# Strassen's scheme for four more token tiles, earlier weight sums, and a last product that ends in parts

## The chip, the cores and the metric

The kernel runs on one core of one Trainium2 chip. A core has five engines that work side by side, each through its own instruction queue: TensorE (PE, matmuls into PSUM banks), VectorE (DVE), ScalarE (ACT), GpSimd (POOL) and SyncE (SP, which here issues nearly all transfers). The metric is the device time of one execution in microseconds; of several runs the median is taken.

## What is computed

Four batches, eight heads, 768 tokens, head size 64. First comes clustered attention: each query and each key is given to the nearest of 16 centroids of its head, and a query sees the keys of its own cluster only. Then a gated feed-forward layer works on all 3072 tokens.

```python
q_assign = np.argmax(np.einsum('bhsd,hcd->bhsc', q_n, c_n), axis=-1)
k_assign = np.argmax(np.einsum('bhsd,hcd->bhsc', k_n, c_n), axis=-1)
mask = q_assign[:, :, :, None] == k_assign[:, :, None, :]
scores = np.where(mask, scale * np.matmul(q, k.transpose(0, 1, 3, 2)), -1e9)
attn_out = softmax(scores) @ v                     # (B, H, S, D)
x = attn_out.transpose(0, 2, 1, 3).reshape(B * S, H * D)
gate = 1.0 / (1.0 + np.exp(-(x @ w_gate)))         # 512 -> 1536
return gate * (x @ w_val) @ w_out                  # 1536 -> 512
```

## The kernel before

**Attention in steps.** The batches b0 to b3 follow each other. The work of attention is cut into 384 steps (96 for each batch): one score matmul of 128 keys by 384 queries (line 788), one exponential on ACT (line 793), three small matmuls into the `av` bank (line 811). Between them stand, at planned steps, what prepares the coming heads: casts and splits of q and k (lines 1353 and 1354), transposes by DMA, cluster logits (`lg`, lines 421 and 434), which DVE reduces to `lgs` (line 449) and to one-hot rows (lines 460 to 469), the sums of v (lines 330 to 346).

**The feed-forward layer as filler.** When a half batch (three token tiles of 128, a block) is through attention, its atoms go into a queue (`ffn_block`): per chunk fc of 12, a gate atom (four matmuls into a bank `g`, line 529, tanh on ACT, line 535) and a value atom (four matmuls into a bank `v`, line 545; DVE then makes the hidden tile `hT`, line 550), and after them the atoms of the output product. At each step `ffn_run(ns)` adds `ns` to a credit and takes atoms from the front of the queue while the credit is positive. The table `SCHED` gives ns for every 24 steps of a batch (`ns10` is the first quarter of batch 1); so it sets how many matmuls of the layer stand beside each step. What is left at the end runs after the last step. The banks `sc`, `g`, `v` and `lg` share a ring of four PSUM banks; two more banks (`op`) hold outputs or transposes (`turns`), two more `av`.

**The output product, plain.** For b0 (`b < PB`, PB = 1) each of the six tiles has twelve matmuls of 512 columns into one bank (line 583), a copy to SBUF on ACT (line 593, tiles 0 and 2 of a block) or DVE (line 591, tile 1) and a store of 256 KB (line 502).

**The output product by Strassen's scheme (Winograd's form).** For b1 to b3 two token tiles and the two halves of the hidden axis make a 2 x 2 block matrix, as do the halves of `w_out` on both axes. Seven products (`steps` in `product_out`) of six matmuls with 256 columns (line 716) stand for eight. It needs four sums of token blocks (class `Sums`, lines 626 to 632, on DVE, made at the chunks that `SUMS_AT` names), four sums of weights (`mix_wo`, line 276, eight instructions on DVE, which go into the held tiles of k, q, v that batch 0 no longer needs, and, last, over the upper right quarter of `w_out`), and sums of products (line 658, DVE; the first one is a copy on ACT, line 662). Two banks, x and y, take the products in turn; a product that starts afresh in a bank waits until the sum of the one before has read it. Tiles (0, 1) of a batch are one product of a single pair, made beside the second block's gates (`aside`); tiles (3, 2) and (4, 5) are one product of two pairs at the batch's end: 84 matmuls, each sum 128 x 512. The last product of the kernel (`final`) stores its parts as they come: the lower tiles, the right half, and, after the seventh product (B21, `end2`), the left half with 128 x 2 x 256.

**Order.** Each engine runs its instructions in the order in which this program issues them. The weights' sums were planned at steps 150 to 170 and 200 to 204; no Strassen product may start before them, and the last of them may not come before the plain products, which read the quarter that it overwrites.

Of the kernel before, what the change touches and what calls it, by code (L numbers as in the profile page):

```python
# [98 lines left out]
def kernel(  # L99
# [163 lines left out]
    HF, HD = NFC // 2, DM // 2  # L263
# [236 lines left out]
    def store(src, b, c0, n, m=slice(0, DM)):  # L500
        def f():
            SP.dma_start(
                out=out[b * S : (b + 1) * S].rearrange("(p c) m -> p c m", c=NCH)[
                    :, c0 : c0 + n, m
                ],
                in_=src,
            )

        d_ = SCHED.get("sd", 0)
        if d_ > 0 and b < B - 2:  # L510
            at(step_no[0] + d_, f)
        else:
            f()

    def ffn_atoms(xT, t0, n, b, final=False):
        blk = t0 // 384
        gv = []
        cost = NDC * max(n, 80) / 2.4 + 3
        pairs = [] if b < PB else [(0, 1)] if blk == 0 else [(3, 2), (4, 5)]
        sm = {x: Sums(b, *x) for x in pairs}  # L520

        def gate(fc, st):
            def f():
                need(("w", fc // WQ, 0), *(("x", b, p, t0 // 128 + c) for p in range(NP) for c in range(n // 128)))
                if fc == 0:
                    HB[b, blk] = htp.tile([128, NFC, 384], HP, name="hT")
                g = bank(512, name="g")
                for dc in range(NDC):
                    PE.matmul(  # L529
                        out=g[:, 0:n], lhsT=wg[fc // WQ][:, dc, fc % WQ, :],  # L530
                        rhs=xT[:, dc, t0 : t0 + n],
                        start=(dc == 0), stop=(dc == NDC - 1),
                    )
                th = thp.tile([128, 384], FP, name="th")
                ACT.activation(th[:, 0:n], g[:, 0:n], AF.Tanh)  # L535
                st.append(th)

            return f

        def val(fc, st):  # L540
            def f():
                need(("w", fc // WQ, 1))
                w = bank(512, name="v")
                for dc in range(NDC):
                    PE.matmul(  # L545
                        out=w[:, 0:n], lhsT=wv[fc // WQ][:, dc, fc % WQ, :],
                        rhs=xT[:, dc, t0 : t0 + n],
                        start=(dc == 0), stop=(dc == NDC - 1),
                    )
                DVE.scalar_tensor_tensor(  # L550
                    HB[b, blk][:, fc, 0:n], st[0][:, 0:n], 1.0, w[:, 0:n], ALU.add, ALU.mult
                )
                for k, x in SUMS_AT[b >= PB, blk].get(fc, []):
                    sm[x].make(k)
                if fc == NFC - 1 and pairs and blk == 0:
                    aside.extend(product_out(b, [sm[(0, 1)]], False))

            return f

        for fc in range(NFC):  # L560
            st = []
            gv.append((cost, gate(fc, st)))
            gv.append((cost, val(fc, st)))
        outs = []
        if b < PB:
            for t in range(n // 128):
                outs += plain_out(b, blk, t)
        elif blk == 1:
            outs = product_out(b, [sm[x] for x in pairs], final)
        return gv + outs  # L570

    def plain_out(b, blk, t):
# [3 lines left out]
        def outp(part):  # L576
# [22 lines left out]

    PB = 1  # L600
    SUMS_AT = {
        (False, 0): {}, (False, 1): {},
        (True, 0): {5: [(3, (0, 1))], 11: [(1, (0, 1)), (2, (0, 1))]},
        (True, 1): {
            1: [(1, (3, 2))], 5: [(2, (3, 2)), (3, (3, 2))], 6: [(3, (4, 5))],
            11: [(1, (4, 5)), (2, (4, 5))],
        },
# [26 lines left out]
    def product_out(b, sums, final):  # L634


        P_ = len(sums)
        st = {}

        def begin():  # L640
            need(*(("wo", i) for i in range(WOP)), *(("wt", i, c) for i in range(4) for c in range(2)))
            slot = taken["op"] % 2
            u = [out_bank() for _ in range(2)]
            x = 0 if slot != taken["last"] else 1
            taken["last"] = (slot + x) % 2
            taken["pair"] = True
            for z, t in (("x", u[x]), ("y", u[1 - x])):
                st[z] = t[:, 0 : P_ * HD].rearrange("p (e m) -> p e m", m=HD)
            if P_ == 1:
                ob = osp.tile([128, 2, DM], FP, name="ob")  # L650
                st["o1"], st["o2"] = ob[:, 0:1], ob[:, 1:2]
            else:
                st["o1"] = osp.tile([128, 2, DM], FP, name="ob")
                st["o2"] = osp.tile([128, 2, DM], FP, name="ob")
            for o in ("o1", "o2"):
                st[o, 0], st[o, 1] = st[o][:, :, 0:HD], st[o][:, :, HD:DM]

        plus = lambda dst, a, z: DVE.tensor_tensor(dst, a, z, ALU.add)  # L658
        C11, C12, C21, C22 = ("o1", 0), ("o1", 1), ("o2", 0), ("o2", 1)

        def end1():
            ACT.activation(st[C11], st["x"], AF.Copy)

        def end4():
            plus(st[C21], st["y"], st[C11])

        def end6():
            plus(st[C12], st["x"], st[C11])

        def end5():  # L670
            plus(st[C22], st["y"], st[C11])
            for m in sums:
                m.make(4)

        def end7():
            plus(st[C21], st["x"], st[C21])
            plus(st[C22], st["x"], st[C22])
            for i, m in enumerate(sums):
                store(st["o2"][:, i], b, m.t2, 1)

        def end3():
            plus(st[C12], st["y"], st[C12])
            if final:
                store(st[C12], b, sums[0].t1, P_, slice(HD, DM))

        def end2():
            plus(st[C11], st["x"], st[C11])
            taken["pair"] = False
            if final:
                store(st[C11], b, sums[0].t1, P_, slice(0, HD))  # L690
            else:
                store(st["o1"], b, sums[0].t1, P_)

        steps = [
            ("x", lambda m: tok(b, m.t1, 0), B11, True, end1),
            ("y", lambda m: tok(b, m.t2, 1), T4, True, end4),
            ("x", lambda m: m.of[2], T2, True, end6),
            ("y", lambda m: m.of[1], T1, True, end5),
            ("x", lambda m: m.of[3], T3, False, end7),
            ("y", lambda m: m.of[4], B22, False, end3),  # L700
            ("x", lambda m: tok(b, m.t1, 1), B21, True, end2),
        ]
        atoms = []
        G = SCHED.get("og", 3)

        def atom(k, e, g):
            z, lhs, rhs, start, end = steps[k]

            def f():
                if k + e + g == 0:  # L710
                    while aside and P_ > 1:
                        aside.pop(0)[1]()
                    begin()
                a = lhs(sums[e])
                for c in range(g, g + G):
                    PE.matmul(  # L716
                        out=st[z][:, e], lhsT=a[:, c, :], rhs=rhs[:, c, :],
                        start=start and c + e == 0, stop=c == HF - 1, skip_group_check=True,
                    )
                if g + G == HF and e == P_ - 1:  # L720
                    end()

            return f

        for k in range(7):
            for e in range(P_):
                for g in range(0, HF, G):
                    atoms.append((G * (HD / 2.4 + 2.5), atom(k, e, g)))
        return atoms

    queue = []
# [609 lines left out]
        plan(f"wo{i}", 44 + 6 * i, lambda i=i: load_wo(i))  # L1341
    for i in range(4):
        for c in range(2):
            plan(f"wt{i}{c}", (150 + 8 * i if i < 3 else 200) + 4 * c, lambda i=i, c=c: mix_wo(i, c))

    def pair_prep(b, p, use):
        st = {}
# [138 lines left out]
```

## Time and profile before

| what | value |
|---|---|
| median of 3 runs (lowest to highest) | 324.65 us (324.54 to 325.34) |
| the profiled execution's own time | 324.9 us |
| its span, first to last instruction | 323.1 us |
| busy in the span | PE 314.7, ACT 231.1, DVE 226.7, POOL 108.6 us |
| granted TensorE clock | 1.0 throughout |
| moved over DMA | 45.15 MB |

PE is the matmul side of TensorE, PEld its weight loads, which run beside the matmuls. A row of a group gives line, engine, operation, result and sources, shape and count; after the bar stand the busy time and the mean of one in ns; after the second bar the engine's idle time just before these instructions and what ended most of it. A matmul's mean holds its whole passage, so that following matmuls overlap; how far apart they start is read from the timeline. In a row of the windows each engine has its busy time in that stretch and, in brackets, its number of instructions. "SPq" are the instructions by which SP issues transfers.

### The profile page before, as it was taken

To read this page: it belongs to the slowest core of one execution; us is meant where nothing else is said; L and a number is where in the kernel's file an instruction comes from. 1 tells how busy PE (TensorE), PEld (TensorE's weight loads), DVE (VectorE), ACT (ScalarE), POOL (GpSimd) and SP (SyncE) were. 2 spreads that over 40 slices of the span, in tenths; PEclk is the share of its full clock that TensorE was granted. 3 is DMA by queue.
4 is the path that set the end of the run, shared out by engine and by line. 5 is a ranking of instruction groups with operands and counts; after the bars stand their busy time and mean duration, and the time that the engine had idled before them with its cause. 6 is when DMAs were issued, how large, how long until landed. Compare 5 with 4: busy or idle time off the path is not lost.

```text
span 323.1 us, 9150 instructions
## 1 busy us (share of the span) xinstructions
PE 314.7 (97%) x3504; PEld 222.1 (69%) x3504; DVE 226.7 (70%) x586; ACT 231.1 (72%) x520; POOL 108.6 (34%) x145
## 2 busy tenths in 40 slices
PE   7999999999999999999999999999999999999994
PEld 5888666766766656666777687666777688667683
DVE  6899656777667997576879688576867356555654
ACT  6688988787899978877867866788777876332310
POOL 5887464154335265433132352423111111000000
PEclk9999999999999999999999999999999999999999
DMA  6999995837987996974784741952503012200103
GB/s 203 384 255 189 244 164 114 200 93 222 251 122 185 159 215 155 248 197 90 107 217 115 233 101 42 311 99 52 111 2 95 34 26 79 77 2 1 67 0 130
DMA packets 77675, 45.15 MB, mean 140 GB/s; under 512 B 56832, under 2 KB 75072, under 8 KB 77632
## 3 DMA queue, kind: packets, MB, share of 16 engines
q1 hardware_dynamic: 73664, 39.73, 49.1%
q0 software_dynamic: 3680, 4.72, 8.9%
q8 instruction: 27, 0.44, 0.6%
q10 hardware_dynamic: 288, 0.13, 0.2%
q14 instruction: 16, 0.13, 0.1%
HBM read 28.34 MB, written 6.29 MB: 107 GB/s over the span
## 4 chain that ended last, share of the span: by engine, by line
PE 87%; DVE 5%; issue 3%; DMA 2%; POOL 1%; SPq 0%; ACT 0%; POOLq 0%; DVEq 0%
PE g L529 19%; PE v L545 19%; PE sc L788 17%; PE av L811 10%; PE o L716 10%; PE o L583 4%; PE lg L434 2%; PE oh_ps L1097 1%; PE lg L421 1%; PE t_ps L1037 1%; DMA xTb<-xp 1%; DMA qraw<-in_q_dram 1%; PE wm L879 1%; DVE ob L658 1%; POOL xp L375 1%
## 5 line engine op out<-in xcount | busy, mean ns | idle before, releaser
L793 ACT ACTIVATE es<-sc 128x384 f16<-128x384 f32 x384 | 174.5, 492 | 40.3 <-PE sc L788 30.9
L788 PE MATMUL sc<-T 128*128 128x384 f16 x384 | 117.8, 326 | 1.0 <-DVE lgs L449 0.6
L811 PEld LDWEIGHTS <-es 128*128 128x128 f16 x1152 | 81.3, 98 | 35.8 <-issue 0.7
L811 PE MATMUL av<-va,es 128*128 128x65 f16 x1152 | 97.5, 194 | 0.0
L550 DVE SCALAR_TENSOR_TENSOR hT<-th,v 128x384 f16<-128x384 f32 x96 | 53.1, 553 | 56.2 <-PE av L811 36.8
L529 PE MATMUL g<-xTb,wg 128*128 128x384 f16 x384 | 78.2, 326 | 0.6 <-DMA xTb<-xp 0.5
L545 PE MATMUL v<-xTb,wv 128*128 128x384 f16 x384 | 78.1, 326 | 0.0
L535 ACT ACTIVATE th<-g 128x384 f32<-128x384 f32 x96 | 47.2, 492 | 33.3 <-PE g L529 14.0
L375 POOL TENSOR_TENSOR xp<-t,rec 128x384 f16<-128x384 f32 (+1 forms) x30 | 21.8, 728 | 100.5 <-DVE rec L372 50.0
L529 PEld LDWEIGHTS <-wg 128*128 128x128 f16 x384 | 37.2, 97 | 19.7 <-issue 0.4
L545 PEld LDWEIGHTS <-wv 128*128 128x128 f16 x384 | 37.4, 98 | 19.0
L788 PEld LDWEIGHTS <-T 128*128 128x128 f16 x384 | 37.1, 97 | 0.6 <-DVE T L1118 0.5
L1354 POOL TENSOR_TENSOR hl<-kraw,hl 128x384 f16<-128x384 f32 x22 | 20.2, 920 | 42.2 <-DVE hl L1353 19.6
L658 DVE TENSOR_TENSOR ob<-o,ob 128x256 f32<-128x256 f32 (+1 forms) x42 | 22.6, 551 | 9.7 <-PE o L716 8.9
L716 PEld LDWEIGHTS <-sum 128*128 128x128 f16 x216 | 20.9, 98 | 5.6 <-DVE sum L632 0.7
L716 PE MATMUL o<-wo,hT 128*128 128x256 f16 x162 | 24.0, 272 | 0.2 <-DVE ob L658 0.2
L1354 POOL TENSOR_TENSOR hl<-qraw,hl 128x384 f16<-128x384 f32 x22 | 20.7, 940 | 10.0 <-DVE hl L1353 9.7
L370 DVE TENSOR_TENSOR t<-av,sv 128x390 f32<-128x390 f32 (+1 forms) x30 | 14.4, 479 | 8.0 <-PE av L811 7.8
L583 PE MATMUL o<-wo,hT 128*128 128x512 f16 x72 | 19.9, 379 | 0.0
L716 PEld LDWEIGHTS <-hT 128*128 128x128 f16 x162 | 15.7, 97 | 4.2 <-issue 0.4
L449 DVE TENSOR_REDUCE lgs<-lg 128x192 f32<-128x384 f32 x23 | 12.7, 551 | 2.7 <-PE lg L434 2.6
L322 POOL CAST va<-vraw 128x768 f16<-128x768 f32 x15 | 12.9, 860 | 2.5 <-DMA vraw<-in_v_dram 2.5
(140 smaller groups left out, 321.9 us busy)
## 6 DMA issues: line engine op xcount, KB each, us to landing
vraw<-in_v_dram SPq DMA_DIRECT2D x15, 384.0 KB, 5.2
kraw<-in_k_dram SPq DMA_DIRECT2D x14, 384.0 KB, 4.1
out_dram<-ob SPq DMA_DIRECT2D x20, 256.0 KB, 2.4
qraw<-in_q_dram SPq DMA_DIRECT2D x12, 384.0 KB, 4.4
wg<-in_moe_w_gate_dram POOLq DMA_DIRECT2D x2, 768.0 KB, 9.1
wv<-in_moe_w_val_dram POOLq DMA_DIRECT2D x2, 768.0 KB, 9.9
wo<-in_moe_w_out_dram POOLq DMA_DIRECT2D x2, 768.0 KB, 8.8
T<-ohT SPq DMA_DIRECT2D x44, 24.0 KB, 1.9
```

Source lines behind the costliest of these rows:

```text
L375: (eng or POOL).tensor_tensor(x, t[:, 0:nq, 0:64], bcast(rec[:, 0:nq], 64), ALU.mult)
L529: PE.matmul(out=g[:, 0:n], lhsT=wg[fc // WQ][:, dc, fc % WQ, :], rhs=xT[:, dc, t0 : t0 + n], start=(dc == 0), stop=(dc == NDC - 1),)
L535: ACT.activation(th[:, 0:n], g[:, 0:n], AF.Tanh)
L545: PE.matmul(out=w[:, 0:n], lhsT=wv[fc // WQ][:, dc, fc % WQ, :], rhs=xT[:, dc, t0 : t0 + n], start=(dc == 0), stop=(dc == NDC - 1),)
L550: DVE.scalar_tensor_tensor(HB[b, blk][:, fc, 0:n], st[0][:, 0:n], 1.0, w[:, 0:n], ALU.add, ALU.mult)
L583: PE.matmul(out=o, lhsT=HB[b, blk][:, fc, bass.ts(t, 128)], rhs=wo[fc // WON][:, fc % WON, :], start=(fc == 0), stop=(fc == NFC - 1),)
L658: plus = lambda dst, a, z: DVE.tensor_tensor(dst, a, z, ALU.add)
L716: PE.matmul(out=st[z][:, e], lhsT=a[:, c, :], rhs=rhs[:, c, :], start=start and c + e == 0, stop=c == HF - 1, skip_group_check=True,)
L788: PE.matmul(out=sc.rearrange("p (c t) -> p c t", t=128), lhsT=s["k"], rhs=s["q"], start=True, stop=True,)
L793: ACT.activation(es, sc, AF.Exp, scale=SCALE)
L811: PE.matmul(out=av[:, a0 + s["c0"] + i, :], lhsT=s["es"][:, bass.ts(i, 128)], rhs=VA[b, p][:, e, s["j"], :], start=(first and i == 0 and a ...
L1354: POOL.tensor_tensor(hl[:, :, 64:128], r, hl[:, :, 0:64], ALU.subtract)
```

## The change

Three things. First, b0 leaves the plain way after its tiles 0 and 1: tiles (3, 2) and (4, 5) go through the product of two pairs as in the other batches, and their token sums are made at the same chunks. Second, the eight weight sums are planned at steps 108, 114, ... 150, and the credits of the quarters change: 490 to 440 ns in the second half of b0, 12 ns more in all of b1, 7 to 8 less in b2. Third, in the last product of the kernel the seventh product no longer accumulates in bank x: three atoms (`closing`) take a ring bank each, for tile 3 with 256 columns and for tile 4 with two parts of 128, add them to the left half and store each part by itself.

```diff
-    300, "ns11": 280, "ns12": 290, "ns13": 265, "ns2": 600, "ns3": 350, "dm0": 7, "dm1": 2,
+    312, "ns11": 292, "ns12": 302, "ns13": 277, "ns2": 600, "ns3": 350, "dm0": 7, "dm1": 2,
...
-    -1, "b1lv1": 0.5, "b1lv2": 0.5, "b1lv3": 1.5, "ns02": 490, "ns03": 490, "ns20": 500,
-    "ns21": 491, "ns22": 481, "ns23": 491, "ns30": 443, "ns31": 443, "ns32": 443, "ns33": 423,
+    -1, "b1lv1": 0.5, "b1lv2": 0.5, "b1lv3": 1.5, "ns02": 440, "ns03": 440, "ns20": 492,
+    "ns21": 484, "ns22": 474, "ns23": 484, "ns30": 443, "ns31": 443, "ns32": 443, "ns33": 423,
...
-        pairs = [] if b < PB else [(0, 1)] if blk == 0 else [(3, 2), (4, 5)]
+        pairs = [(3, 2), (4, 5)] if blk else [] if b < PB else [(0, 1)]
...
-                for k, x in SUMS_AT[b >= PB, blk].get(fc, []):
+                for k, x in SUMS_AT[blk].get(fc, []) if pairs else []:
...
-        if b < PB:
-            for t in range(n // 128):
+        if blk == 1:
+            outs = product_out(b, [sm[x] for x in pairs], final)
+        elif b < PB:
+            for t in range(2):
                 outs += plain_out(b, blk, t)
-        elif blk == 1:
-            outs = product_out(b, [sm[x] for x in pairs], final)
...
         def end2():
             plus(st[C11], st["x"], st[C11])
             taken["pair"] = False
-            if final:
-                store(st[C11], b, sums[0].t1, P_, slice(0, HD))
-            else:
-                store(st["o1"], b, sums[0].t1, P_)
+            store(st["o1"], b, sums[0].t1, P_)
...
+        def closing(e, a, z):
+            def f():
+                o = bank(z - a, name="o_end")
+                lhs = tok(b, sums[e].t1, 1)
+                for c in range(HF):
+                    PE.matmul(
+                        out=o, lhsT=lhs[:, c, :], rhs=B21[:, c, a:z],
+                        start=c == 0, stop=c == HF - 1,
+                    )
+                m = st["o1"][:, e, a:z]
+                plus(m, o, m)
+                store(m.unsqueeze(1), b, sums[e].t1, 1, slice(a, z))
+
+            return f
+
-        for k in range(7):
+        for k in range(6 if final else 7):
             for e in range(P_):
                 for g in range(0, HF, G):
                     atoms.append((G * (HD / 2.4 + 2.5), atom(k, e, g)))
+        if final:
+            for e, a, z in ((0, 0, HD), (1, 0, HD // 2), (1, HD // 2, HD)):
+                atoms.append((900, closing(e, a, z)))
...
-            plan(f"wt{i}{c}", (150 + 8 * i if i < 3 else 200) + 4 * c, lambda i=i, c=c: mix_wo(i, c))
+            plan(f"wt{i}{c}", 108 + 12 * i + 6 * c, lambda i=i, c=c: mix_wo(i, c))
```

More of the change, by code (lines that the diff above doesn't have):

```diff
@@ L601 @@
     SUMS_AT = {
-        (False, 0): {}, (False, 1): {},
-        (True, 0): {5: [(3, (0, 1))], 11: [(1, (0, 1)), (2, (0, 1))]},
-        (True, 1): {
+        0: {5: [(3, (0, 1))], 11: [(1, (0, 1)), (2, (0, 1))]},
+        1: {
             1: [(1, (3, 2))], 5: [(2, (3, 2)), (3, (3, 2))], 6: [(3, (4, 5))],
```

## The prediction

> **What bounds the kernel now.** I read the page first, then the groups by shape, the chain of waits, the windows by stage and the timeline of the end. The page and its chain name the matrix engine:
>
> ```profile
> span 323.1 us, 9150 instructions
> PE 314.7 (97%) x3504; PEld 222.1 (69%) x3504; DVE 226.7 (70%) x586; ACT 231.1 (72%) x520; POOL 108.6 (34%) x145
> PE 87%; DVE 5%; issue 3%; DMA 2%; POOL 1%; SPq 0%; ACT 0%; POOLq 0%; DVEq 0%
> PE g L529 19%; PE v L545 19%; PE sc L788 17%; PE av L811 10%; PE o L716 10%; PE o L583 4%; PE lg L434 2%; PE oh_ps L1097 1%; PE lg L421 1%; PE t_ps L1037 1%; DMA xTb<-xp 1%; DMA qraw<-in_q_dram 1%; PE wm L879 1%; DVE ob L658 1%; POOL xp L375 1%
> ```
>
> PE is busy 97% of the span and is 87% of the chain that ended last; no other engine passes 72%. A microsecond of PE work taken out anywhere between the lead-in and the end should therefore come off the time, unless an engine that is full for a while makes PE wait. Where that can be is read from the windows; I cut them at attention steps 48, 96, 108, 132, 150, 168 and 192 (a step is one score matmul of line 788):
>
> ```profile
> core 0: us, PE busy (x) PEld busy (x) DVE busy (x) ACT busy (x) POOL busy (x), PEclk, DMA share, GB/s
> 35.80:73.30 37.50, 37.39 (x434) 25.12 (x433) 25.61 (x68) 32.44 (x75) 16.63 (x20) 1.00 0.74 160
> 73.30:80.50 7.20, 7.20 (x81) 4.46 (x80) 5.30 (x13) 5.60 (x13) 3.03 (x4) 1.00 0.79 228
> 80.50:95.20 14.70, 14.70 (x193) 10.13 (x192) 8.40 (x24) 13.13 (x31) 5.66 (x7) 1.00 0.84 184
> 95.20:104.90 9.70, 9.70 (x118) 6.59 (x117) 7.65 (x24) 8.85 (x21) 4.53 (x5) 1.00 0.96 186
> 104.90:116.30 11.40, 10.83 (x129) 7.11 (x128) 11.08 (x25) 9.40 (x23) 5.09 (x6) 1.00 0.83 176
> 116.30:129.10 12.80, 12.80 (x154) 7.98 (x152) 10.86 (x31) 10.75 (x26) 7.16 (x9) 1.00 0.80 172
> ...
> 104.90:116.30 11.40, 3.42 (x4) 1.00 0.83 176
> 116.30:129.10 12.80, 1.17 (x2) 1.00 0.80 172
> ```
>
> (The last two rows are line 276 alone, the weights' sums.) PE is full in every stretch but one. In 104.9 to 116.3 us DVE is busy 11.08 of 11.40 us, four weights' sums with 3.42 us among them, and there PE idles 0.57 us. That is the price this trace shows for a full DVE, and the waits name it:
>
> ```profile
> PE sc L788 <- DVE lgs L449: 0.6, 1, 0.6
> PE g L529 <- DMA xTb<-xp: 0.5, 1, 0.5
> PE o L716 <- DVE ob L658: 0.2, 1, 0.2
> ```
>
> **Part 1: the product of the first batch.** By the instruction order of both programs, 48 matmuls of 512 columns (line 583, four tiles of twelve) leave and 84 of 256 columns come (seven products, two tiles, six chunks). What each costs is read from spacing, since the mean of a matmul holds its whole passage through the array:
>
> ```profile
> 68.38 0.86 PE o L583 x4
> 69.75 0.86 PE o L583 x4
> ...
> 311.96 1.47 PE L716 MATMUL o<-qheld,sum 128*128 128x256 f16 x12
> 313.27 1.47 PE L716 MATMUL o<-kheld,sum 128*128 128x256 f16 x12
> ```
>
> Four wide ones take 0.86 us, 0.215 each. Twelve narrow ones start 1.31 us before the next twelve, 0.109 each. So 48 x 0.215 = 10.3 us go and 84 x 0.109 = 9.2 us come: **-1.17 us** of PE work. The 36 further weight loads lie beside the matmuls: a load takes 97 to 98 ns (groups below), less than the 109 ns of a narrow matmul. Exposed, they would cost 36 x 0.098 = 3.5 us; that is a rival.
>
> The Trainium skill, "TensorE: Matmul & The Clock Gate", section "Back-to-back issue gap", speaks against this part: it gives a sustained 131 ns for 512 columns and 81 ns for 128, by which 48 wide ones cost 6.3 us and 84 short ones at least 6.8, so the product would lose 0.5 us or more instead of gaining. The rows here do not bear it out (0.215 us for a wide one in the interleaved stretch).
>
> The other engines' share, by groups:
>
> ```profile
> L658 DVE TENSOR_TENSOR ob<-o,ob 128x512 f32<-128x512 f32 x21 | 14.1, 688 | 9.6 <-PE o L716 8.9 <-ACT es L793 0.7
> L550 DVE SCALAR_TENSOR_TENSOR hT<-th,v 128x384 f16<-128x384 f32 x96 | 53.1, 553 | 56.2 <-PE av L811 36.8 <-PE v L545 18.8
> L716 PEld LDWEIGHTS <-sum 128*128 128x128 f16 x216 | 20.9, 98 | 5.6 <-DVE sum L632 0.7
> L626 DVE TENSOR_TENSOR sum<-hT 128x768 f16<-128x768 f16 x9 | 5.9, 650 | 0.2
> L628 DVE TENSOR_TENSOR sum<-sum,hT 128x768 f16<-128x768 f16 x9 | 5.5, 606 | 0.3
> L630 DVE TENSOR_TENSOR sum<-hT 128x768 f16<-128x768 f16 x9 | 5.2, 576 | 0.1
> L632 DVE TENSOR_TENSOR sum<-hT,sum 128x768 f16<-128x768 f16 x9 | 4.7, 550 | 0.0
> L593 ACT ACTIVATE ob<-o 128x512 f32<-128x512 f32 x4 | 2.4, 600 | 0.2
> L591 DVE COPY ob<-o 128x512 f32<-128x512 f32 x2 | 1.4, 688 | 0.0
> L276 DVE TENSOR_TENSOR qheld<-wo,kheld 128x768 f16<-128x768 f16 x2 | 1.2, 584 | 0.0
> L276 DVE TENSOR_TENSOR wo<-wo,qheld 128x768 f16<-128x768 f16 x2 | 1.1, 552 | 0.0
> ```
>
> ACT loses three copies and gains one (-1.2 us). DVE gains seven sums of outputs and eight of tokens and loses one copy: 6 x 0.688 + 2 x (0.650 + 0.606 + 0.576 + 0.550) = +8.9 us, in steps 107 to 191. On SP four stores of 256 KB become two of 256 and one of 512 KB; behind the last stand transposes and loads for the next batch, issued tens of steps ahead, so a late store costs nothing there.
>
> **Part 2: the weights' sums earlier, the pace.** Eight sums move from steps 150 to 204 to steps 108 to 150. They must come before the new product starts at step 158; their inputs are ready (the second half of the weights long loaded, the held tiles free after the first quarter, the last plain output at step 107). The changed pace moves 6,144 columns of gate and value work out of steps 48 to 96, into steps 96 to 192: PE work that changes place. It costs something only where another engine then ends last. In 35.8 to 73.3 us PE's 37.4 us shrink by 6,144 / 2,348 per us (256 columns in 0.109 us) = 2.6 to 34.8; ACT has 32.4 there, so PE still ends last.
>
> For DVE I add the instructions that the order moves into each stretch to its busy time. Steps 108 to 132: 8.4 + 3.7 = 12.1 of 14.7 us, room. Steps 132 to 150: three token sums, two qheld, one wo and one head's reduction come in, about 4.4 us by their means, 0.4 to 0.6 less as they overlap in a queue; 7.65 + 3.9 = 11.5 against a stretch of 9.7 + 0.65 us (more columns): DVE is **1.2 us over**, 1.7 without overlap. Steps 150 to 168, full before, lose 5.0 and gain 2.4: that 0.57 us wait goes. Steps 168 to 192: 10.86 + 4.4 less overlap = 14.8 against 13.6: again 1.2 over, but with almost no hT in it, only output sums that have one product step (12 matmuls spread over five steps) to spare. What queues behind a late sum on DVE is the hT that frees a ring bank of `v` and the `lgs` that frees one of `lg`; PE waits once the ring of four has come round, so not the whole overrun is paid. A lower end is 0; an upper end is the overrun, 1.7 + 1.6. The nearest row (97% full, 0.57 us) is small, so I take 0.7 for the first, 0.3 for the second, minus the 0.57 that goes: **+0.45 us**.
>
> **Part 3: the last product in parts.** The end of the timeline:
>
> ```profile
> 316.00 1.48 PE L716 MATMUL o<-wo,sum 128*128 128x256 f16 x12
> 316.33 1.89 DVE L658 TENSOR_TENSOR ob<-o,ob 128x512 f32<-128x512 f32 x3
> 317.64 2.63 SPq L502 DMA_DIRECT2D out_dram<-ob  x4
> 317.66 1.47 PE L716 MATMUL o<-wo,hT 128*128 128x256 f16 x12 [0.18 <-DVE ob L658]
> 319.17 0.69 DVE L658 TENSOR_TENSOR ob<-o,ob 128x512 f32<-128x512 f32 x1 [0.96 <-PE o L716]
> ...
> L502 SPq DMA_DIRECT2D out_dram<-ob x22: 332/374/877, 71.3 to 319.9; - x22
> DMA to landing us min/median/max: 2.0/2.4/5.7
> ...
> L490 SPq DMA_DIRECT2D T<-ohT x44: 507/540/1176, 78.5 to 250.5; - x44
> DMA to landing us min/median/max: 1.8/1.9/3.4
> ```
>
> In a ring bank the last twelve need not wait for DVE: they start at 316.00 + 1.31 = 317.31 instead of 317.66. Cut as 256, 128 and 128 columns, the last sum is a quarter of the old one; it can end near 319.1 instead of 319.86. But then SP is late next: two stores wait from 317.6, one from 318.2, then three small ones, six issues of 0.33 to 0.37 us with gaps. Back to back from 317.64 the sixth ends at 319.9 to 320.3; the fourth now ends at 317.64 + 2.63 = 320.27. So of 0.75 us on DVE, 0 to 0.4 reaches the queue. The last transfer is 64 KB instead of 256. From the issue's end, 256 KB land in 2.0 - 0.33 = 1.7 us at best and 24 KB in 1.8 - 0.5 = 1.3; 64 KB save 0.1 to 0.35. I take 0.15 + 0.25: **-0.4 us**, between -0.1 and -0.75.
>
> **Sum.** -1.17 + 0.45 - 0.4 = -1.1 us. The profiled execution took 324.9 us (span 323.1 and 1.8 around it), the median of the runs is 324.65, 0.25 less; against the median this gives **323.5 us**. About 0.3% (1.0 us) is what a measurement here can tell from no change: below 323.7 counts as faster, above 325.6 as slower.
>
> **Rivals.**
> - *Given back.* DVE's overruns are paid nearly whole in the first stretch: 1.7 + 0.6 - 0.57 = +1.7; with -1.17 and -0.4 that is 324.8; with the second stretch unpaid, 324.2. For it: the wait of `sc` on `lgs`. Against: only 0.57 us at 97%.
> - *VectorE becomes the bound.* If the ring gives PE no slack at all, both overruns are paid: 1.7 + 1.6 - 0.57 = +2.7, in all +1.15, **325.8 us**, slower. It decides as soon as PE waits as long in steps 132 to 192 as DVE is over. Against: DVE idles 56.2 us ahead of hT over the whole run, waiting for PE, so it mostly starts such a stretch without arrears.
> - *No new wait.* The sums fit, the old 0.57 goes, the end brings 0.6: 324.65 - 1.17 - 0.57 - 0.6 = 322.3.
> - *Short matmuls are not cheaper.* 36 exposed weight loads: +3.5, in all 324.65 - 1.17 + 3.5 - 0.4 + 0.45 = 327.0. Twelve narrow ones in 1.31 us, loads included, speak against it. (The page's rule named above ends on this side of zero too.)
> - That the change does not do what it says is excluded: the order shows the matmuls replaced.
>
> **How the numbers follow.** My forecast 0.60 (its own range 322.9 to 324.1; 0.42 of it below 323.7), given back 0.19, VectorE the bound 0.10, no new wait 0.09, short matmuls 0.02. Faster: 0.42 + 0.09 = 0.51. Slower: 0.08 of the third, 0.02 of the fifth and 0.01 of the second = 0.11. Within: 0.38. The range 322.4 to 324.9 leaves out the slower cases (0.12) and the tails of two others (0.07).
>
> **What would show it.** In the new profile: 24 matmuls left at line 583 and 84 more of 256 columns at 0.109 apart; PE idle in steps 132 to 168 named by hT or `lgs`, 0.5 to 1.2 us; no wait of `o` on `ob` in the last product; six stores at the end, the last issue ending at 319.9 to 320.3 less what came before it. Wrong would be: PE idle of 2 us or more in that stretch, ACT named as releaser in steps 60 to 96, or a last store that lands as late after its issue as the old one.

## The result, and the profile after

The changed kernel takes **327.76 us** (median of 4 runs, 326.97 to 329.21) beside 324.6 us for the kernel before on the same chip: a ratio of 1.0100, 95% interval 1.0078 to 1.0122. It is slower by 1%; 323.5 had been forecast, with a range up to 324.9. The profiled execution took 327.84 us. Its page:

```profile
span 326.0 us, 9230 instructions
PE 315.6 (97%) x3546; PEld 226.0 (69%) x3546; DVE 235.4 (72%) x602; ACT 230.7 (71%) x518; POOL 108.3 (33%) x145
PE 84%; DVE 6%; ACT 4%; DMA 3%; issue 1%; POOL 1%; ACTq 0%; DVEq 0%; POOLq 0%
```

A first look misleads: PE is busy 97% of the span as before. But busy time is not work. A matmul's record also holds the time that it stands in the pipeline (326 ns for 384 columns, where the next one can start after 162), so a matmul that starts late still shows a busy PE, and PE's busy time did not fall by the 1.2 us of work that the change takes out. The chain says it better: PE carries 84% of it instead of 87%, ACT, which had none, 4%, DVE 6% instead of 5%, DMA 3% instead of 2%. The windows, cut at the same steps as before:

```profile
35.70:71.70 36.00, 35.47 (x424) 24.14 (x422) 24.38 (x64) 31.08 (x73) 15.75 (x19) 1.00 0.84 149
71.70:79.90 8.20, 8.12 (x86) 4.82 (x84) 7.14 (x17) 6.93 (x15) 3.51 (x4) 1.00 0.81 229
79.90:94.80 14.90, 14.66 (x194) 10.13 (x192) 11.64 (x29) 12.29 (x29) 6.44 (x7) 1.00 0.63 171
94.80:106.60 11.80, 11.00 (x121) 6.83 (x119) 11.49 (x29) 9.03 (x22) 3.92 (x4) 1.00 0.76 199
106.60:118.00 11.40, 10.89 (x144) 8.21 (x143) 10.07 (x26) 9.63 (x23) 4.71 (x6) 1.00 0.66 127
118.00:133.60 15.60, 14.07 (x185) 11.15 (x184) 15.19 (x38) 11.25 (x25) 7.57 (x10) 1.00 0.65 134
```

Columns: stretch, length, then busy time and count of PE, PEld, DVE, ACT and POOL, the granted clock, the DMA share and GB/s. The fourth row (steps 132 to 150) has DVE busy 11.49 of 11.80 us, the last (168 to 192) 15.19 of 15.60. Those are the two stretches that the prediction called 1.2 us over; both grew until DVE fitted in.

The matmuls themselves are as forecast: 24 are left at line 583, and each of the 84 new ones is followed by the next matmul within 0.112 us, 9.15 us for all of them.

**A ledger of lost time.** To compare stretches with different work I take each one's length, between the starts of two score matmuls, and subtract PE's work: every matmul in program order at its usual spacing in a full stream of these traces (0.162 us for 384 columns, 0.216, 0.109 and 0.056 for 512, 256 and 128, 0.029 for `av`, 0.025 for `lg`). What remains is time that PE lost. Four kernels, two of them experiments told of below (f1: load on DVE alone; f3: the changed credits alone, called the pace):

| steps | work before | work after | lost before | lost after | lost f1 | lost f3 |
|---|---|---|---|---|---|---|
| 0 to 48 | 23.88 | 23.88 | 2.96 | 2.77 | 2.75 | 2.83 |
| 48 to 96 | 36.48 | 33.89 | 1.02 | 2.12 | 1.01 | 1.96 |
| 96 to 108 | 7.09 | 7.74 | 0.09 | 0.46 | 0.09 | 0.34 |
| 108 to 132 | 14.36 | 14.36 | 0.33 | 0.54 | 0.32 | 0.65 |
| 132 to 150 | 9.37 | 10.02 | 0.11 | 1.80 | 0.11 | 0.48 |
| 150 to 168 | 10.70 | 10.62 | 0.91 | 0.77 | 0.91 | 0.91 |
| 168 to 192 | 12.68 | 13.49 | 0.12 | 2.16 | 2.19 | 0.12 |
| 192 to 216 | 18.94 | 18.30 | 0.16 | 0.40 | 0.16 | 0.40 |
| 216 to 288 | 55.01 | 55.01 | 1.48 | 0.63 | 1.19 | 0.44 |

Behind step 288 before and after are alike (1.11 lost up to step 383) except for the end, which is 0.45 us shorter. So the 2.85 us by which the span grew are: work -1.20, the end -0.45, lost time +4.5. Of that, 3.6 lie in steps 132 to 192 (1.69, -0.14, 2.04), 1.7 in steps 48 to 132, and 0.85 comes back in steps 216 to 288. That last figure is the least sure: e1, f1, f2, e8 and e9, which run the same instructions there as the kernel before, lose 1.05 to 1.28 where its trace shows 1.48. f3, with the pace alone, loses 0.44.

**Where the lateness went.** The waits of PE after the change (total, times, longest):

```profile
PE g L529 <- DMA xTb<-xp: 0.8, 1, 0.8
PE g L529 <- DVE hT L550: 0.8, 2, 0.5
...
PE g L529 <- ACT es L807: 0.4, 1, 0.4
...
PE o L712 <- DVE ob L657: 0.4, 1, 0.4
PE lg L434 <- DMA T<-hl: 0.3, 1, 0.3
```

Of these, the list of before has only the one on `xTb` (0.5) and the one on `ob` (0.2). They sum to 2.7 us, less than the 4.5 of the ledger: the list counts a wait only from the end of PE's last record. In steps 132 to 150 five gates and values start 0.23 to 0.55 us late by their spacing, 1.6 us together, and only one stands in the list (0.4). Four of the five are put down to ACT, one to DVE; why ACT is named there, at 9.03 of 11.80 us, was not settled. The chain of waits (start, length, what) is DVE with short pauses from 98.66 us on, for 8.7 us. It ends just behind the stretch and where the prediction had looked, at an `hT` with a gate behind it that starts 0.68 us late:

```profile
98.66 0.06 DVE va L330
...
106.25 0.49 DVE t L370
...
106.87 0.54 DVE hT L550
...
107.45 0.32 PE g L529
```

In steps 168 to 192 the chain shows a way that the prediction had not followed:

```profile
117.95 0.90 POOL hl L1368
...
118.87 5.10 DMA T<-hl
...
124.02 0.47 PE lg L434 x12
...
127.69 1.28 DVE ob L657 x2
128.97 0.28 DVE t L370
...
129.27 0.18 DVE rec L372
129.45 0.26 DVE hl L1367
...
129.74 0.10 POOL xp L375
...
130.02 0.06 POOL hl L1368
130.09 3.01 DMA xTb<-xp
...
133.14 0.32 PE g L529
```

Read it from below. The first gate of the next block needs the transposed x, and the transposition takes 3.01 us. It waits for POOL's product `xp`, that for DVE's reciprocal `rec` and sum `t`, and `t` stood in DVE's queue behind two output sums of the new product. At the top the same happens to a key transpose, 5.10 us of DMA, with the logits behind it. (That transposition itself is as long without the product's sums, 5.38 us in e10.) So a late DVE does not reach PE only when a PSUM ring comes round: it also reaches it through transfers. The product hides only part of this one. Its last twelve matmuls had waited for the sums too, and are through at 131.4 us; the next filler is the gate, whose fourth matmul waits:

```profile
129.03 0.49 PE L712 MATMUL o<-wo,hT 128*128 128x256 f16 x3 [0.37 <-DVE ob L657]
...
133.14 0.32 PE L529 MATMUL g<-xTb,wg 128*128 128x384 f16 x1 [0.84 <-DMA xTb<-xp]
```

By spacing the three waits of this stretch, `lg` on the key transpose, `o` on the sums and the gate, cost 0.48, 0.54 and 1.01 us.

**The end**, by its timeline:

```profile
319.29 1.48 PE L712 MATMUL o<-wo,sum 128*128 128x256 f16 x12
319.62 1.89 DVE L657 TENSOR_TENSOR ob<-o,ob 128x512 f32<-128x512 f32 x3
320.61 1.49 PE L726 MATMUL o_end<-wo,hT 128*128 128x256 f16 x18
320.93 2.85 SPq L502 DMA_DIRECT2D out_dram<-ob  x6
321.47 0.96 DVE L657 TENSOR_TENSOR ob<-o_end,ob 128x256 f32<-128x256 f32 x3
```

The last matmuls start 1.32 us after the twelve ahead of them, with no wait on `ob` (1.66 before). DVE ends 3.14 us after 319.29 (before: 3.86 after 316.00), but SP's six issues end 4.49 us after it, its four 4.27 before. The gain is in what follows the last issue: 326.0 - 323.78 = 2.2 us to the end of the span, 323.1 - 320.27 = 2.8 before.

### The profile page after: what moved, and what is told of

Read it like the earlier page. It is cut to its first block, busy times and chain, and to the rows that moved or that the text cites. A ratio compares the mean times of both kernels' runs of the same rounds, so it can differ in the third digit from the quotient of the medians.

```text
span 326.0 us, 9230 instructions
## 1 busy us (share of the span) xinstructions
PE 315.6 (97%) x3546; PEld 226.0 (69%) x3546; DVE 235.4 (72%) x602; ACT 230.7 (71%) x518; POOL 108.3 (33%) x145
## 4 chain that ended last, share of the span: by engine, by line
PE 84%; DVE 6%; ACT 4%; DMA 3%; issue 1%; POOL 1%; ACTq 0%; DVEq 0%; POOLq 0%
PE v L545 18%; PE g L529 18%; PE sc L802 16%; PE o L712 13%; PE av L825 9%; PE lg L434 2%; ACT es L807 2%; PE o L583 2%; DMA T<-hl 2%; PE lg L421 1%; DVE hT L550 1%; PE t_ps L1051 1%; PE oh_ps L1111 1%; DMA xTb<-xp 1%; DVE hl L1367 1%
## 5 line engine op out<-in xcount | busy, mean ns | idle before, releaser
L657 DVE TENSOR_TENSOR ob<-o,ob 128x512 f32<-128x512 f32 (+1 forms) x48 | 26.5, 566 | 8.4 <-PE o L712 7.2
L712 PEld LDWEIGHTS <-sum 128*128 128x128 f16 x264 | 25.7, 98 | 6.4 <-DVE sum L631 0.2
L712 PE MATMUL o<-wo,hT 128*128 128x256 f16 x186 | 28.4, 272 | 0.4 <-DVE ob L657 0.4
L712 PEld LDWEIGHTS <-hT 128*128 128x128 f16 x186 | 18.0, 97 | 5.2 <-issue 0.6
L434 PE MATMUL lg<-cm,T 128*128 128x32 f16 x288 | 11.4, 177 | 0.5 <-DMA T<-hl 0.3
```

What stands on the lines that cost most here:

```text
L434: PE.matmul(out=lg[:, bass.ts(i, 32)], lhsT=t[:, c, :], rhs=cm[:, h].rearrange("p s n -> p (s n)"), start=True, stop=True,)
L712: PE.matmul(out=st[z][:, e], lhsT=a[:, c, :], rhs=rhs[:, c, :], start=start and c + e == 0, stop=c == HF - 1, skip_group_check=True,)
```

## Experiments

**Theory:** the sums of the new product and the weights' sums load DVE beyond what the stretches hold, and PE pays the overrun; beside it the lowered pace makes ACT late in steps 48 to 96. **Rivals:** the product's own order of dependent matmuls and sums costs the time, whatever DVE's load; the short matmuls are dearer than their spacing; the end lost. All ratios are to the kernel before, run on the same chip in the same series; between the series its median lay at 324.37 to 324.52 us.

**The end alone** (e1). The kernel before with `closing` and the new `end2`, nothing else.

> The kernel before with the last product in three ring-bank parts and nothing else. If the end of the new kernel is worth what its trace shows (0.3 us earlier last matmul, 0.2 us less behind it), 0.4 to 0.5 us come off: 324.1 to 324.3 us. The other theory, that six stores instead of four on SP give it all back, expects no change: 324.6 us.

324.07 us, ratio 0.9990 (0.9981 to 0.9999, 11 runs): -0.3 us, somewhat less than the 0.4 to 0.5 expected. The end gains, and is not the cause.

**DVE's work taken out** (e2, e10). In e2 the changed kernel uses token blocks of the first batch in place of their eight sums; e10 leaves out four of the product's seven output sums in this batch as well. Both leave out a part of the computation, with the same matmuls in the same order.

```diff
             a2 = lambda f: tok(self.b, self.t2, f)
+            if self.b < PB:
+                self.of[i] = a1(0) if i in (2, 3) else a2(0) if i == 1 else a1(1)
+                return
...
         def end7():
-            plus(st[C21], st["x"], st[C21])
-            plus(st[C22], st["x"], st[C22])
+            if b >= PB:
+                plus(st[C21], st["x"], st[C21])
+                plus(st[C22], st["x"], st[C22])
```

(The second part, and the same in `end3` and `end2`, is e10 alone.)

> The changed kernel without the eight token sums of batch 0 on VectorE (the product takes the token tiles themselves in their place, so that part of the computation is changed; the matmuls are the same ones). Theory V, VectorE is the bound in steps 132 to 150 and 168 to 192: 4.8 us of its work go, the 1.8 and 2.2 us that PE lost there fall by 2 us or more together: 325.0 to 325.8 us. Theory P, the new pace causes the loss and VectorE is busy beside it: 0.5 us at most come off, 327.2 us or more.

> The changed kernel without the eight token sums and without the last four of the seven output sums of batch 0's large product (so these parts of the computation are left out; all matmuls and stores stay). Theory V: with 7.5 of 8.9 us of the added VectorE work gone, the 4.0 us that PE lost in steps 132 to 150 and 168 to 192 fall below 1 us and the product's 1.2 us of matmul time show: 323.6 to 324.3 us. If the wait for the transposed x at step 190 has another cause than VectorE, 0.5 us or more stay there: 324.6 us and above.

e2: 324.85 us, 1.0019 (1.0009 to 1.0029). e10: 324.44 us, 1.0002 (0.9992 to 1.0012). Against 1.0100 with all sums, 4.8 us less on DVE brought 2.6 us, and 7.5 us less brought 3.2: e2 comes out as theory V had expected, e10 between its two expectations. In e2 steps 132 to 150 lose 0.95 us and 168 to 192 lose 0.73; in e10 0.95 and 0.32. Its windows of these two stretches:

```profile
94.40:105.40 11.00, 10.55 (x121) 6.90 (x120) 10.69 (x28) 9.03 (x22) 4.15 (x5) 1.00 0.76 198
116.20:130.00 13.80, 13.77 (x187) 11.13 (x185) 11.00 (x31) 11.41 (x25) 6.94 (x10) 1.00 0.80 169
```

In the second DVE is down to 11.00 of 13.80 and PE is full again. In the first it is still busy 10.69 of 11.00: three weights' sums and a head's preparation fill it even without the product's sums. The 84 matmuls stayed, at 9.15 us in e10 as in the changed kernel, so they are not the cause. Their waits for the sums went together with the sums, so the rival of the product's own order needs another test.

**DVE's load put in** (f1, f2). The counter-test, on the kernel before, which keeps its plain product: eight sums of 128 x 768 that nothing reads, at steps 168 to 189 (f1) or at 108 to 129 (f2).

```diff
+    def load_dve(k):
+        t = sump.tile([128, HF, 128], HP, tag="sum", name="sum")
+        o = t.rearrange("p (a e) m -> p a (e m)", e=2)
+        c = slice(3 * (k % 2), 3 * (k % 2) + 3)
+        DVE.tensor_tensor(o, B21[:, c], B22[:, c], ALU.add)
+
+    for k in range(8):
+        plan(f"ld{k}", 168 + 3 * k, lambda k=k: load_dve(k))
```

> The kernel before with eight further sums of 128 x 768 on VectorE at steps 168, 171 ... 189; nothing reads them, and the product of the first batch stays plain. Before, VectorE is busy 10.86 of 12.80 us between steps 168 and 192; eight sums of some 0.6 us make it 15.1 to 15.7, 2.3 to 2.9 more than the stretch holds. If VectorE's load itself makes the matrix engine late (theory), that stretch loses 1.5 to 2.5 us and the time is 325.4 to 326.8 us. If it was the order of the product and its sums (rival), the stretch loses less than 0.4 us and the time stays at 324.2 to 324.8.

> The same eight sums at steps 108, 111 ... 129, where VectorE of the kernel before is busy 8.40 of 14.70 us: 13.2 with them. If only load beyond what a stretch holds costs something (theory), steps 108 to 132 lose at most 0.3 us more and the time is 324.2 to 324.8. If every sum that is queued delays the matrix engine wherever it stands (rival), it costs 1 us or more: 325.4 and up.

f1: 326.42 us, 1.0054 (1.0034 to 1.0073). f2: 324.57 us, 1.0007 (0.9992 to 1.0022). The stretch of each, f1's first:

```profile
116.10:131.00 14.90, 13.25 (x154) 8.18 (x153) 14.51 (x35) 11.52 (x27) 7.09 (x9) 1.00 0.65 149
```

```profile
79.50:94.70 15.20, 14.98 (x194) 10.15 (x193) 12.27 (x30) 13.11 (x31) 6.54 (x7) 1.00 0.65 175
```

In f1 the stretch lost 2.19 us instead of 0.12, nearly the 2.16 that the change itself lost there, with not one matmul altered. In f2 the same sums found 12.27 of 15.20 us busy and cost 0.47 us in the stretch (0.3 had been expected at most) and nothing that can be measured in the time. So load is enough, and nearly all of the cost is for load above what the stretch holds. In f1 the waits name `sc` behind `lgs`, not the transfers (0.6 of this stands in steps 150 to 168, as in the kernel before):

```profile
PE sc L788 <- DVE lgs L449: 2.2, 3, 1.2
```

Another instruction was late than in the changed kernel, and the bill was nearly the same.

**The pace** (f3, e3, e11). f3 is the kernel before with the changed credits alone; e3 the changed kernel with 470 in place of 440 and the old ones in the second batch; e11 the changed kernel with four copies moved from ACT to DVE.

```diff
-    300, "ns11": 280, "ns12": 290, "ns13": 265, "ns2": 600, "ns3": 350, "dm0": 7, "dm1": 2,
+    312, "ns11": 292, "ns12": 302, "ns13": 277, "ns2": 600, "ns3": 350, "dm0": 7, "dm1": 2,
...
-    -1, "b1lv1": 0.5, "b1lv2": 0.5, "b1lv3": 1.5, "ns02": 490, "ns03": 490, "ns20": 500,
-    "ns21": 491, "ns22": 481, "ns23": 491, "ns30": 443, "ns31": 443, "ns32": 443, "ns33": 423,
+    -1, "b1lv1": 0.5, "b1lv2": 0.5, "b1lv3": 1.5, "ns02": 440, "ns03": 440, "ns20": 492,
+    "ns21": 484, "ns22": 474, "ns23": 484, "ns30": 443, "ns31": 443, "ns32": 443, "ns33": 423,
```

(f3; in e11 the entries `r2ev0E`, `r2ev1E`, `g1ev0E` and `g0pl1E`, each "A", leave the table.)

> The kernel before with the changed paces alone (440 ns in the second half of the first batch, 12 ns more in the second batch, 7 to 8 less in the third). If the lowered pace by itself makes ScalarE the bound in steps 48 to 96 (theory), that stretch loses 2.0 to 2.2 us instead of 1.02 and the time is 325.0 to 325.8. If the loss came with the product's other instructions (rival), the stretch loses at most 1.4 and the time is 324.2 to 324.8.

> The changed kernel with 470 ns instead of 440 in the second half of batch 0 and the old pace in batch 1, so that the filler stands beside steps 48 to 96 and 96 to 192 nearly as before the change. Theory P: the 1.1 us more that PE lost in steps 48 to 96 come back and part of the later loss too: 325.8 to 326.6 us. Theory V: VectorE's work in steps 96 to 192 is the same, so PE loses there what it has less to do; at most the 1.1 us of steps 48 to 96 move into steps 96 to 192: 327.3 to 328.2 us.

> The changed kernel with four copies out of PSUM in steps 60 to 90 (two of 384 and two of 768 columns) on VectorE instead of ScalarE: 2.6 us less for ScalarE, 1.8 us more for VectorE, which has 5 us of room there. If ScalarE ends last in steps 48 to 96 since the pace was lowered, the 2.1 us that PE loses there fall to 1.3 or less: 326.8 to 327.2 us. If not, no change or, through VectorE's order, slower: 327.7 us and above.

f3: 325.37 us, 1.0026 (1.0015 to 1.0038): slower by 0.85 us, with 1.96 us lost in steps 48 to 96 (after: 2.12, before: 1.02). This is a net: in its trace steps 48 to 150 lose 1.9 us more than before, and steps 216 to the end 1.6 less. e3: 326.62 us, 1.0071 (1.0057 to 1.0084), at the upper end of what theory P, the pace, had expected. Steps 48 to 96 lose 1.42 and steps 132 to 150 1.06 instead of 1.80; against it, 96 to 108 lose 1.09 instead of 0.46, and 168 to 192 2.67 instead of 2.16, where the transposition of x takes 3.58 us instead of 3.01 and the wait on `xTb` grew from 0.8 to 1.4. e11: 327.06 us, 1.0089 (1.0070 to 1.0109), 1.63 lost in steps 48 to 96, where 1.3 or less had been expected. The chain of waits of the changed kernel in that stretch:

```profile
64.08 0.37 DVE hl L1367
...
64.46 0.53 ACT es L807
64.99 0.38 ACT th L535
65.38 0.38 ACT es L807
...
65.78 0.80 ACT T L999
...
66.61 0.50 ACT es L807
...
67.15 0.32 PE sc L802
```

Before, the chain from 60 to 70 us is PE without a gap; three of its pieces:

```profile
63.96 0.34 PE t_ps L920 x6
64.30 0.65 PE g L529 x4
64.94 0.09 PE av L811 x3
```

In the changed kernel the copy `T` of 0.80 us stands in ACT's queue between exponentials that PE waits for, 2.6 us of ACT in a row; f3, without the product, has the same pieces from 64.37 us on, and `T` with the same 0.80. So the pace does cost, by itself: over the whole stretch ACT is busy only 31.08 of 36.00 us, but for 3 us it is the bound. That is one part of the 1.1 us: by spacing the score matmul behind this chain is 0.30 us late, another 0.35 is a wait of the logits on a DVE copy at 58.27 us, as in f3, and the rest is spread. e11, which takes `T` and three more copies off ACT, took 0.5 us of the loss away; its 0.4 us of the time lies within the intervals.

**Relief by moving work** (e4, e5, e12, e6, e7). e4: the weights' sums at steps 76 to 113; e5: the next block 3.5 steps later; e12: both. e6: both and e3's credits. e7: e6, and the token sums 1 to 3 of the first batch's two pairs, six of eight, on POOL.

```diff
-            plan(f"wt{i}{c}", 108 + 12 * i + 6 * c, lambda i=i, c=c: mix_wo(i, c))
+            plan(f"wt{i}{c}", (76 + 10 * i if i < 3 else 108) + 5 * c, lambda i=i, c=c: mix_wo(i, c))
...
-            lag = SCHED.get(f"lag{key}{i}", 8)
+            lag = SCHED.get(f"lag{key}{i}", 8) + (3.5 if (b, i) == (1, 0) else 0)
...
+            eng = POOL if self.b < PB else DVE
             if i == 1:
-                DVE.tensor_tensor(o, a2(0), a2(1), ALU.add)
+                eng.tensor_tensor(o, a2(0), a2(1), ALU.add)
```

> The changed kernel with the first six weights' sums planned at steps 76 to 101 and the last two at 108 and 113. Theory V: 4.0 us of VectorE work leave steps 108 to 150 for steps 76 to 101, where it had about 3 us of room; the 1.8 us lost in steps 132 to 150 fall below 0.7, the 2.2 us in steps 168 to 192 stay: 326.4 to 327.0 us. Theory P: no change, 327.8 us.

> The changed kernel with the first block of batch 1 let into the queue 3.5 steps later, so that its first gate stands at step 192, as before the change, instead of 190. If the matrix engine's wait for the transposed x there (0.8 us, 1.0 by spacing) comes from beginning two steps early on top of a late VectorE, it goes: 326.7 to 327.1 us. If VectorE's lateness alone sets it, the same time is lost in another wait: 327.5 to 327.9 us.

> The changed kernel with the weights' sums at 76 to 113 and the first block of batch 1 from step 192, but its own pace. Alone they brought 1.2 and 1.35 us. If the losses are separate places, 2.5 us: 325.0 to 325.4 us. If what one relieves the other no longer can, since both are VectorE's arrears reaching the transposed x, 1.5 us or less: 326.2 us and above.

> The changed kernel with the three relaxations together: 470 ns in the second half of batch 0 and the old pace in batch 1, the weights' sums at 76 to 113, the first block of batch 1 from step 192. If the three losses are separate places, 1.1, 1.2 and 0.8 us add up: 324.5 to 325.0 us. If they are one thing, VectorE's total work over steps 96 to 192, the sum is smaller: 325.5 us or more. In both cases it does not beat the kernel before by more than 0.3%.

> The kernel of the three relaxations with six of batch 0's eight token sums on GpSimd instead of VectorE (GpSimd has 25 us of work in the 56 us of steps 96 to 192). If what is left of the loss is VectorE's work, another 1 to 1.5 us go: 323.5 to 324.2 us, below the kernel before. Against it: a GpSimd sum takes longer (0.92 us for half as many elements), it stands in order before the low halves of q and k and the normalised x, and the two engines slow each other; if that decides, 326 us or more.

| run | us | ratio (95%) | lost 96 to 108 | 132 to 150 | 168 to 192 | 192 to 216 |
|---|---|---|---|---|---|---|
| e4 | 326.56 | 1.0069 (1.0055 to 1.0082) | 1.13 | 0.82 | 1.57 | 0.39 |
| e5 | 326.41 | 1.0060 (1.0045 to 1.0075) | 0.46 | 1.80 | 1.30 | 0.30 |
| e12 | 325.97 | 1.0046 (1.0033 to 1.0059) | 1.13 | 0.82 | 1.29 | 0.16 |
| e6 | 327.33 | 1.0093 (1.0076 to 1.0110) | 1.58 | 0.89 | 0.90 | 1.6 |
| e7 | 332.14 | 1.0236 (1.0218 to 1.0254) | 1.58 | 4.45 | 1.45 | 1.2 |

e4 halves the loss in steps 132 to 150 and pays 0.67 us of it in 96 to 108, where DVE becomes full instead (8.63 of 8.86 us); steps 150 to 168 lose 0.15 instead of 0.77, and 168 to 192 also less. e5 gives the transposition time. Together (e12) they bring 1.8 us of the 3.2, less than their sum. e6 and e7 are misses: they were to be the best, and lost more. In e6 the wait on `xTb` is back: the product's last matmuls start at 130.10 us, the block's first gate at 131.19, and the transposition, issued at 128.87, takes 4.21 us. The early weights' sums stand ahead of instructions that PE needs at once:

```profile
PE g L529 <- DMA xTb<-xp: 1.3, 1, 1.3
PE oh_ps L1206 <- DVE T L947: 0.7, 1, 0.7
PE g L529 <- DVE xTb L854: 0.7, 1, 0.7
```

In e7 POOL takes three times as long for a sum as DVE (a mean of 1794 ns instead of 606), and DVE and PE wait: one score matmul waits 2.0 us for `hT`. One group of it:

```profile
L626 POOL TENSOR_TENSOR sum<-hT 128x768 f16<-128x768 f16 x2 | 3.6, 1794 | 2.1 <-DVE hT L550 2.1
```

**A part that gains** (e8, e9). e8 is the kernel before with six of the eight weights' sums moved to steps 108 to 138 (the last two, which may not come before the plain products, to 194 and 200); e9 adds the end of e1.

```diff
-            plan(f"wt{i}{c}", (150 + 8 * i if i < 3 else 200) + 4 * c, lambda i=i, c=c: mix_wo(i, c))
+            plan(f"wt{i}{c}", (108 + 12 * i if i < 3 else 194) + 6 * c, lambda i=i, c=c: mix_wo(i, c))
```

> The kernel before with six of the eight weights' sums at the changed kernel's steps 108 to 138 (the last two stay at 194 and 200, since the plain products still read what they overwrite) and nothing else. If the early sums by themselves crowd VectorE in steps 132 to 150, about 1 us is lost there: 325.0 us or more. If it is the product's token and output sums that fill it, the early sums cost nothing and take the 0.8 us wait of steps 162 to 168 away: 323.6 to 324.1 us.

> The kernel before with two parts of the change alone: the last product in three ring-bank parts and six of the eight weights' sums at steps 108 to 138; no product for batch 0 and the old pace. The two single runs came off by 0.3 and 0.9 us at places that do not touch (the end, and steps 150 to 168), so both add up: 323.1 to 323.5 us. If the early sums' gain was another kernel's wait that moved by chance, less than 0.6 us in all: 324.0 us.

e8: 323.58 us, 0.9975 (0.9963 to 0.9986). e9: 323.58 us, 0.9978 (0.9966 to 0.9989). Both beat both kernels by 0.7 to 0.8 us or more. In e8 the loss in steps 150 to 168 falls from 0.91 to 0.15, and no other stretch pays: steps 108 to 132 had the room. The end's 0.3 us do not show on top in e9's median, which misses the 323.1 to 323.5 expected. In its trace the part behind step 383 is 0.37 us shorter than e8's, but the part up to step 48, whose matmuls are the same in all kernels, is 0.46 longer (it takes 34.8 to 36.3 us in the kept traces); whether that hides the gain in the median too is not settled.

## Why the prediction was wrong

- **Part 1, -1.17 us of matmul work:** right. The ledger's work falls by 1.20 us at the spacings that the prediction took, and the 84 new matmuls kept theirs (9.15 us). The Trainium skill's sustained gaps ("TensorE: Matmul & The Clock Gate", section "Back-to-back issue gap": 131 ns for 512 columns, 81 for 128) do not fit these traces: matmuls of 512 columns start no closer than 214 ns, those of 128 mostly 56 ns apart.
- **Part 2, VectorE, +0.45 us: this step failed.** It measured +3.6 us (1.69, -0.14, 2.04). That DVE would be over in exactly the stretches 132 to 150 and 168 to 192 was right, and so about was by how much. What failed is "PE waits once the ring of four has come round, so not the whole overrun is paid", and with it the choice of 0.7 and 0.3 us between 0 and 1.7 and 1.6 after "the nearest row (97% full, 0.57 us)". That row was misread as well: 0.57 is idle time by the records, and by spacing that stretch lost 0.91. The overrun was paid whole, and in the second stretch more than whole. That DVE "idles 56.2 us ahead of hT over the whole run" was a sum over other stretches. And "almost no hT in it", the reason for a small second term, looked at the ring alone: the late instructions were `t`, `rec` and `hl`, whose results go through POOL and a transposition of 3.0 to 5.1 us to PE. For steps 168 to 192, f1 shows that the load suffices, and e2 and e10 that it is what the product adds. In steps 132 to 150 the product's sums are half of it: without them (e10) 0.95 of the 1.80 is still lost, with the weights' sums alone (e8) 0.14, with the pace alone (f3) 0.48.
- **The pace, at nothing:** wrong. It was weighed by sums over 37.5 us (PE 34.8, ACT 32.4), but ACT is the bound for some 3 us within them, and a DVE copy is late too. f3 shows +0.85 us in the time, the balance of larger losses and of gains in the later batches. The prediction had named ACT as releaser in steps 60 to 96 as a sign of being wrong, and it came, though it explains only a part of the stretch's loss.
- **The wait in steps 150 to 168, -0.57 us:** it goes in e2 to e4, e6 to e10 and e12 (0.10 to 0.25 lost there); in the changed kernel lateness from the stretch before takes its place (0.77). e8 shows that the move of the weights' sums alone was worth 0.8 to 0.9 us, more than the 0.57 that the forecast gave it.
- **Part 3, -0.4 us:** right in size (-0.45 in the trace, -0.3 measured), and right that SP's issues are the limit. The division was off: the issues end 0.2 us later than before, and the time behind the last issue, with a smaller transfer in it, is 0.6 shorter.
- **The rivals:** "VectorE becomes the bound" (0.10, 325.8 us) is what happened, with its deciding point met, and 2 us larger. The ledger has 3.6 instead of its 2.7 in steps 132 to 192, and outside of them, where the rival had nothing, 1.1 in steps 48 to 96 and 0.6 in 96 to 132, less what comes back later.

## What to carry to other kernels

Set each added instruction against the spare time of its own engine in the stretch where it runs; once the sum passes the stretch's length, take the overrun as paid in full unless a row shows what absorbs it. Follow a late engine through the transfers that its results feed, to the first instruction of the next block, and look for stretches of a few microseconds in which another engine is the bound: sums over 30 us hide them. And when a change has several parts, try each alone: here a move of six instructions was a gain that the product beside it buried.

## What the runs showed of the hardware

A DVE sum with two sources in SBUF (128 x 768, f16) takes 0.55 us, but at times 0.6 to 1.3. In both kernels, and in f1 and f2, each of those above 0.6 had started while a POOL instruction was running, and ended 0.41 to 0.42 us after that one's end. Here is one of the changed kernel, POOL's instruction and then DVE's (it ends at 106.24, POOL's at 105.84):

```profile
104.92 0.92 POOL L1368 TENSOR_TENSOR hl<-kraw,hl 128x384 f16<-128x384 f32 x1 [1.94 <-issue]
...
105.16 1.08 DVE L276 TENSOR_TENSOR wo<-wo,qheld 128x768 f16<-128x768 f16 x1
```

The Trainium skill says so ("SBUF — State Buffer", section "Who interferes with whom"): a DVE instruction with two SBUF inputs contends with a GpSimd instruction that reads SBUF, over a shared pair of ports that is an exclusive lock. The trace agrees: the later DVE sum ends 0.41 us after POOL's instruction. The prediction counted these sums at their mean; where they meet POOL's work, in steps 132 to 168, the group of line 276 has them at twice that:

```profile
L276 DVE TENSOR_TENSOR wo<-wo,qheld 128x768 f16<-128x768 f16 x2 | 2.3, 1174 | 0.0
```

Many stretches whose instructions did not change repeat to within some 0.05 us from kernel to kernel (steps 288 to 383: 67.46 us in before, after, f1 and f2 alike; steps 48 to 96: 37.49 to 37.50 in before, e1, f1, f2, e8 and e9), so there a ledger can tell tenths of a microsecond apart, which the medians can't. Others do not: steps 0 to 48 take 26.42 to 27.35 us over all kernels, and steps 216 to 288 take 56.07 to 56.50 in the kernels that run the same instructions there.
